# Attention and two gated layers on one core: the order of the first loads, the stores of the split sums, and 16 more dummy products

## The chip, the core and the metric

The kernel runs on one core of a Trainium2 chip. The metric is the device time of one execution in microseconds (us), here the median of the runs. TensorE (PE) multiplies matrices, VectorE (DVE), ScalarE (ACT) and GpSimd (POOL) work element by element, and SyncE (SP) issues nearly all DMAs. Each engine takes its instructions strictly in the order of its own queue, so an instruction that waits holds back all that stands behind it on its engine.

## What is computed

Attention with a bias from a running sum, then two feed-forward layers (shapes: 4 batches, 8 heads, 576 positions, 64 per head; 2304 tokens of width 512):

```python
scores = scale * np.matmul(q, k.transpose(0, 1, 3, 2))
cum = np.cumsum(np.maximum(s, 0.0), axis=-1)
bias = -(cum[:, :, :, None] - cum[:, :, None, :])
scores = np.where(causal, -1e9, scores + np.minimum(bias, 0.0))
attn = softmax(scores)                      # max, exp, sum + 1e-9
x = (attn @ v), heads side by side          # 2304 x 512
h = np.maximum(np.maximum(x @ w1, x @ w2), x @ w3); x = h @ w_out
a = x @ w_a; b = x @ w_b; out = (a * b) @ w_out2
```

## The kernel before

**Tiling.** Attention works on pairs of heads. A stage is one batch and one half of the positions (R = 0: the first 256, R = 1: the other 320), with four pairs each, so there are eight stages and 32 pairs. A pair's operands k and q are loaded with the bias as two more rows: row 64 of the k tile and row 65 of the q tile hold the running sum `cum`, so that one product per block gives scores with bias (`f_unit0`, `f_unit`, `f_joint`; the products are f and fj). The first three stages are done in this plain way. From the fourth stage on (20 pairs) q, k and `cum` are split into a rounded part and a remainder, and two products are added (`smm`); the split `cum` comes from two DRAM arrays, `kt` and `qt`, through `k_tails` and `q_tails` into the tiles KB2 and QA2.

**One pair.** TensorE makes the scores (f), DVE adds the mask and takes the maximum (L430), ACT takes the exponential (L437), DVE the reciprocal of the sum (L441, L442), POOL multiplies by it (L447), TensorE transposes the block (ft, L540), ACT copies it out (L543), TensorE multiplies with v (fpv, L563), ACT and DVE split the result into Xh and Xl (L81, L92).

**The first layer beside it.** The gates (g, L624) are matrix products of Xh and Xl with weights w1, w2, w3. Each block of weights (wraw, 512 KB) is loaded by SP (L230) into one of three buffers and then converted: ACT (L241), DVE (L244, L245), POOL (hg, L88), DVE (lg, L92). A buffer is free for the next load when its lg is done. I call the blocks W0, W1, W2 and so on in the order of their loads.

**The start.** `load_first` loads k and q of pairs 1 to 4 (kq0, 264 KB each; in the code p = 0 to 3, and tiles kraw for the first two pairs and kqv for the others), then copies the bias rows out of `cum`, one row per tile on SP's queue (L368) and one on ACT's (L369), then loads v and weights. A row's copy waits until its pair's operands have landed, since they go into the same tile. `tails` (`store_tails`, L176) then rounds `cum` (ACT, L181), takes the remainder (POOL, L182) and stores `cum` and both parts to DRAM in 15 DMAs. Ahead of all that, `spin(16)` runs 16 dummy products of the identity with itself on TensorE; two to four more stand behind each step of the first four pairs.

**What sets the order.** The code is traced with priorities, and `stream` gives every piece of attention, of the first layer and of the weights a place; a scheduler then fixes one order for each engine. `issue_after(x)` puts an instruction behind x on x's engine. A DMA has one of eight completion counters in turn and waits for the DMA that had the counter before it.

Of the kernel before, what the change touches and what calls it, by code (L numbers as in the profile page):

```python
# [8 lines left out]
F32 = mybir.dt.float32  # L9
# [20 lines left out]
def kernel(  # L30
# [18 lines left out]
    nc = tc.nc  # L49
# [10 lines left out]
    P = 128  # L60
# [7 lines left out]
    Q0 = 256  # L68
# [6 lines left out]
    def f(ap):  # L75
        return ap.bitcast(F32)
# [53 lines left out]
    SR = s.shape[0]  # L130
    ck = dram.tile([SR, 2, S], F32, name="ck")
    cq = dram.tile([SR, 2, N1], F32, name="cq")
    kt = dram.tile([SR, 2, 2, S], F32, name="kt")
    qt = dram.tile([SR, 2, 2, N1], F32, name="qt")
    x2T = dram.tile([DM, NT], F32, name="x2T")

    def pt_tile(shape, dt, nm):
# [31 lines left out]
    for h in range(2):  # L169
# [3 lines left out]
            op0=ALU.mult, op1=ALU.add,  # L173
        )

    def store_tails():  # L176
        chl = [
            mp.tile([SR, KC * N1], F32R, tag=f"X{c}1", bufs=1, name=f"c{c}")
            for c in "hl"
        ]  # L180
        nc.scalar.copy(chl[0][:, : 2 * S], cum)  # L181
        nc.gpsimd.tensor_tensor(  # L182
            chl[1][:, : 2 * S], cum, f(chl[0][:, : 2 * S]), op=ALU.subtract
        )
        for (dk, dq, t) in (
            (ck, cq, cum),
            (kt[:, 0], qt[:, 0], f(chl[0])),
            (kt[:, 1], qt[:, 1], f(chl[1])),
        ):
            a, b = parts(t)  # L190
            nc.sync.dma_start(dk[:, :, :Q0], a)
            nc.sync.dma_start(dk[:, :, Q0:], b)
            nc.sync.dma_start(dq[:, 0], b[:, 0])
            nc.sync.dma_start(dq[:, 1, 0:64], b[:, 1, 256:])
            nc.sync.dma_start(dq[:, 1, 64:], b[:, 1, :256])


    KB1 = ap_.tile([P, 2, S], F32R, name="KB1")
# [102 lines left out]
        return 2 * b + R < NPLAIN  # L301

    rows_in = []

    def pair_tiles(b, p, R):
        nk = Q0 if R == 0 else S
# [24 lines left out]
    def load_v(qv, nq, vn):  # L331
        return nc.sync.dma_start(vn, qv[:, 2 * nq :])

    def load_pair(b, p, R):

        nk = Q0 if R == 0 else S
        nq = Q0 if R == 0 else N1
        nb = 5 if R else 2
        bp = b * NP + p
        qv = (qv1 if R else qv0)[b, p]  # L340
        kt_, qt_, kn, qn, vn = pair_tiles(b, p, R)
        if is_plain(b, R):
            if R:
                nc.sync.dma_start(kn[0:66], k1[bp])
                nc.sync.dma_start(qn[0:66], q1[bp])
                nc.sync.dma_start(kn[64:65], ck[bp : bp + 1])
                nc.sync.dma_start(qn[65:66], cq[bp : bp + 1])
            else:
                load_kq0(bp, kt_)
                row = ck[bp : bp + 1, :, :Q0]  # L350
                nc.sync.dma_start(kn[64:65], row)
                nc.sync.dma_start(qn[65:66], row)
            load_v(qv, nq, vn)
        else:
            nc.sync.dma_start(qt_[:, : 2 * nq + nb * P], qv)
            for r in (0, 64):
                nc.sync.dma_start(kn[r : r + 64], kT[b, p, :, :, 0:nk])
        return kn, qn, vn.rearrange("p (b f) -> p b f", f=P)

    def load_first():  # L360

        first = [pair_tiles(0, p, 0) for p in range(NP)]
        for p in range(NP):
            load_kq0(p, first[p][0])
        for p in range(NP):
            kn, qn = first[p][2:4]
            row = parts(cum)[0][p : p + 1]
            k_ = nc.sync.dma_start(kn[64:65], row)  # L368
            q_ = nc.scalar.dma_start(qn[65:66], row)  # L369
            rows_in.append(k_.ins)  # L370
        for p in range(NP):
            with tc.issue_after(rows_in[NP - 1]):
                if p:
                    fetch_w1(w1_keys[p - 1])
                load_v(qv0[0, p], Q0, first[p][4])
        return [
            (kn, qn, vn.rearrange("p (b f) -> p b f", f=P))
            for _, _, kn, qn, vn in first
        ]
# [4 lines left out]
        return (p % 2) * (S // 2) if R == 0 else 0  # L384

    def k_tails(b, p, R):
        nk = Q0 if R == 0 else S
        ko = koff(R, p)
        nc.sync.dma_start(f(KB2[0:2, :, ko : ko + nk]), kt[b * NP + p, :, :, :nk])

    def q_tails(b, p, R):
        nq = Q0 if R == 0 else N1
        nc.sync.dma_start(
            heads(f(QA2), 2, 4, nq), (qt if R else kt)[b * NP + p, :, :, :nq]
        )

    def split_qk(b, p, R, kn, qn):
        nk = Q0 if R == 0 else S
# [297 lines left out]
    def do_split(i):  # L696
        if split_pair(i):
            b, R, p = pairs[i]
            q_tails(b, p, R)
            if not k_early(i):  # L700
                k_tails(b, p, R)
            split_qk(b, p, R, *nat_of[i][:2])

    def attn_pieces(i, X):
        b, R, p = pairs[i]
        st = {}
        out_ = []

        def add(cost, fn):
            out_.append((cost, fn))  # L710

        def nxt():
            do_split(i + 1)

        def pv():
            f_x(R, p, f_pv(R, st["PT"], nat_of.pop(i)[2]), *X())
            ahead(i + 2)

        def nop():
            pass  # L720

        plain = is_plain(b, R)
        def prep():
            st["PT"] = pt_tile([P, 2, 4 * N1], F32, "PF")

        add(0, prep)

        def do_t(u, h, pj=None):
            t_unit(st["PT"], h, u, st[u, h], pj)

        if R == 0:
            for h in range(2):
                if plain:
                    add(700, lambda h=h: st.__setitem__(h, f_unit0(*nat_of[i][:2], h, i < 4)))
                else:
                    add(550, lambda h=h: st.__setitem__(h, s_unit0(p, h)))
            if i < NP:
                add(0, lambda: spin(4))
            add(0, nxt)
            add(DLY0, nop)  # L740
            for h in range(2):
                add(330, lambda h=h: f_t0(st["PT"], h, st[h]))
                if i < NP:
                    add(0, lambda: spin(2))
            add(DLY1, nop)
            add(700, pv)
        else:
            def su(u, h):
                if plain:
                    add(900, lambda: st.__setitem__((u, h), f_unit(*nat_of[i][:2], h, u)))  # L750
                else:
                    add(600, lambda: st.__setitem__((u, h), s_unit(p, h, u)))

            add(1040, lambda: st.__setitem__("J", f_joint(*nat_of[i][:2]) if plain else s_joint(p)))
            su(2, 0)
            su(3, 0)
            su(3, 1)
            add(DLY2, nop)
            add(440, lambda: t_joint(st["PT"], st["J"]))
            add(440, lambda: do_t(2, 0, st["J"]))  # L760
            su(2, 1)
            add(0, nxt)
            add(440, lambda: do_t(3, 0))
            add(440, lambda: do_t(3, 1))
            add(330, lambda: do_t(2, 1))
            add(DLY3, nop)
            add(2200, pv)
        return out_
# [69 lines left out]
            store_tails()  # L838

    stream.append((0.1, 0, tails))  # L840
    stream.append((0.5, 0, preset))

    def w_next():
# [721 lines left out]
```

## Time and profile before

| | us |
|---|---|
| runs shown | 916.93, 917.34, 920.71 |
| median of the runs | 917.34 |
| the profiled execution's own time | 921.83 |
| span in its profile (first to last instruction) | 920.0 |
| outside the span | 1.83 |

All rows below are of the profiled execution. Its own time is 4.49 us above the median of the runs. The profile gives time from the span's start; "idle" is the time in which an engine stood still ahead of an instruction, and behind the arrow stands what ended it. TensorE's granted clock is given as a share of 2.4 GHz, so 1.00 is 2.4 and 0.50 is 1.2 GHz. A product in 32-bit floats has two records.

### The profile page before, as it was taken

Reading aid. Unit: us, or ns where it says so; the run is one execution under the profiler, and the core shown is the slowest. Engines: PE = TensorE matmul, PEld = TensorE weight load, DVE = VectorE, ACT = ScalarE, POOL = GpSimd, SP = SyncE. Lnnn points to the kernel's source line nnn. Section 1 sums busy time; section 2 is a strip of 40 time slices with the busy share of each in tenths; the row PEclk is TensorE's granted clock in tenths of the full one; section 3 lists DMA queues with packets and bytes.
Section 4 is the critical chain, followed back from the end, with each engine's and each line's share of the span. In section 5 each row is a group of like instructions: output and inputs, shape, how many; then the busy total and the mean of one; then the engine's idle time right before and its main releaser. Section 6 shows DMA issues by size and latency. Waiting matters only on the chain.

```text
span 920.0 us, 17159 instructions
## 1 busy us (share of the span) xinstructions
PE 904.3 (98%) x6296; PEld 849.0 (92%) x6296; DVE 595.9 (65%) x1407; ACT 380.7 (41%) x879; POOL 230.7 (25%) x328
## 2 busy tenths in 40 slices
PE   7999999999999999999999999999999999999998
PEld 6577889998999989999899999999999998999998
DVE  6688534555445554456469567777675868896874
ACT  4565643655446554456433332223222223423321
POOL 7554311322223222223122102111111212321211
PEclk9899999999999999999999999999999999999999
DMA  6655332213222123231134214444443234254331
GB/s 178 203 189 175 95 88 83 85 54 90 80 82 87 54 77 92 57 104 61 35 108 168 73 60 151 147 164 145 152 144 121 103 125 144 76 162 154 122 115 46
DMA packets 55212, 102.36 MB, mean 111 GB/s; under 512 B 5736, under 2 KB 39432, under 8 KB 55128
## 3 DMA queue, kind: packets, MB, share of 16 engines
q1 hardware_dynamic: 50392, 96.53, 33.3%
q10 hardware_dynamic: 4736, 4.73, 1.6%
q8 instruction: 50, 0.82, 0.4%
q14 instruction: 34, 0.28, 0.1%
HBM read 77.29 MB, written 23.94 MB: 110 GB/s over the span
## 4 chain that ended last, share of the span: by engine, by line
PE 90%; DVE 4%; DMA 3%; issue 1%; POOL 1%; ACT 1%; SPq 0%; POOLq 0%; DVEq 0%; ACTq 0%
PE g L624 24%; PE X L1111 23%; PE Z L1111 11%; PE o L652 8%; PE fpv L563 6%; PE Y L1111 6%; PE t L577 3%; PE f L498 2%; PE s L454 1%; PE s L455 1%; PE ft L540 1%; DVE slot L922 1%; DMA qvraw<-in_qv_dram 1%; PE tj L590 1%; PE fj L498 1%
## 5 line engine op out<-in xcount | busy, mean ns | idle before, releaser
L624 PE MATMUL g<-Xl,hg 128*128 128x256 f32 (+1 forms) x576 | 175.1, 305 | 0.0
L624 PE MATMUL g<-Xh,hg 128*128 128x256 f32 (+1 forms) x576 | 174.3, 305 | 0.5 <-ACT xo L657 0.5
L624 PE MATMUL g<-Xh,lg 128*128 128x256 f32 (+1 forms) x576 | 173.7, 302 | 0.0
L624 PEld LDWEIGHTS g<-Xl,hg 128*128 128x128 f32 x576 | 109.4, 190 | 4.0 <-issue 2.0
L624 PEld LDWEIGHTS g<-Xh,hg 128*128 128x128 f32 x576 | 108.9, 190 | 3.1 <-issue 0.8
L624 PEld LDWEIGHTS g<-Xh,lg 128*128 128x128 f32 x576 | 109.3, 190 | 2.0 <-issue 1.4
L1111 PE MATMUL X<-xh,wh 128*128 128x384 f32 x288 | 97.5, 339 | 1.5 <-ACT u L1154 0.6
L1111 PE MATMUL X<-xl,wh 128*128 128x384 f32 x288 | 96.9, 336 | 0.0
L1111 PE MATMUL X<-xh,wl 128*128 128x384 f32 x288 | 96.9, 337 | 0.0
L88 POOL TENSOR_SCALAR wh<-wval 128x256 fp32r<-128x256 f32 x84 | 41.7, 505 | 181.7 <-DVE wval L916 135.2
L1111 PE MATMUL X<-woh,slot 128*128 128x256 f32 x432 | 81.1, 281 | 0.5 <-ACT ob L1154 0.5
L633 DVE TENSOR_TENSOR hf<-g,hf 128x256 f32<-128x256 f32 (+1 forms) x96 | 43.6, 454 | 45.7 <-PE g L624 42.9
L447 POOL TENSOR_SCALAR P<-P,rs 128x128 f32<-128x128 f32 (+2 forms) x80 | 49.6, 624 | 88.3 <-DVE rs L442 73.3
L922 DVE TENSOR_TENSOR slot<-hraw,slot 128x768 fp32r<-128x768 f32 x60 | 60.5, 1032 | 14.9 <-POOL slot L88 14.0
L1111 PEld LDWEIGHTS X<-woh,slot 128*128 128x128 f32 x432 | 68.0, 189 | 0.7 <-ACT ob L1154 0.7
L922 DVE TENSOR_TENSOR u<-Z,u 128x384 f32<-128x384 f32 x72 | 39.6, 552 | 44.5 <-ACT u L1154 34.1
L437 ACT ACTIVATE P<-P,nm 128x128 f32<-128x128 f32 (+2 forms) x80 | 46.6, 583 | 32.9 <-DVE nm L430 26.8
L1111 PE MATMUL X<-wol,slot 128*128 128x256 f32 x216 | 60.1, 280 | 0.0
L652 PE MATMUL o<-hl,ho 128*128 128x256 f32 (+1 forms) x192 | 57.9, 303 | 0.0
L652 PE MATMUL o<-hh,ho 128*128 128x256 f32 (+1 forms) x192 | 57.6, 304 | 0.3 <-ACT xo L657 0.3
L652 PE MATMUL o<-hh,lo 128*128 128x256 f32 (+1 forms) x192 | 57.7, 304 | 0.0
L1111 PEld LDWEIGHTS X<-xh,wh 128*128 128x128 f32 x288 | 54.1, 188 | 3.0 <-ACT u L1152 1.1
(165 smaller groups left out, 2252.9 us busy)
## 6 DMA issues: line engine op xcount, KB each, us to landing
hT<-u SPq DMA_DIRECT2D x72, 192.0 KB
hraw<-hT SPq DMA_DIRECT2D x36, 384.0 KB
wraw<-in_moe_w_dram SPq DMA_DIRECT2D x18, 512.0 KB
wraw<-in_moe_w_out_dram SPq DMA_DIRECT2D x18, 512.0 KB
qvraw<-in_qv_dram SPq DMA_DIRECT2D x12, 640.0 KB
kraw<-in_kT_dram SPq DMA_DIRECT2D x24, 288.0 KB
wraw<-in_moe_w_a_dram SPq DMA_DIRECT2D x12, 512.0 KB
wraw<-in_moe_w_b_dram SPq DMA_DIRECT2D x12, 512.0 KB
```

Source lines behind the costliest of these rows:

```text
L88: nc.gpsimd.tensor_scalar(o, i, scale, 1.0, op0=ALU.mult, op1=ALU.mult)
L437: e_ = nc.scalar.activation(pt[:, c0:c1], pt[:, c0:c1], AF.Exp, bias=first, scale=-1.0, accum_out=sm[:, g : g + 1],)
L447: nc.gpsimd.tensor_scalar(pt[:, c0:c1], pt[:, c0:c1], rs[:, g : g + 1], 1.0, op0=ALU.mult, op1=ALU.mult,)
L454: nc.tensor.matmul(ps, QA1[:, qs], KB1[:, h, ksl], start=True, stop=False)
L498: nc.tensor.matmul(o, qn[0:66, h, q0 : q0 + m], kn[0:66, h, k0:k1], start=True, stop=True)
L563: nc.tensor.matmul(ps[h * D : h * D + D, c0:n], w, x, start=(t == 0), stop=(t == len(mm[h]) - 1),)
L577: nc.tensor.transpose(ps[:, j * P : j * P + P], pt[:, j * P : j * P + P], ident)
L624: nc.tensor.matmul(ps[:, :n], w[:, kk, :], x[:, kk, :], start=(i == 0), stop=(i == len(mm) - 1),)
L633: st["V"] = nc.vector.tensor_tensor(hf, ps[:, :n], hf, op=ALU.max)
L652: nc.tensor.matmul(ps[:, :n], w[:, c, :], x[:, m, :n], start=(i == 0), stop=(i == len(mm) - 1),)
L922: return {"V": nc.vector, "P": nc.gpsimd}[e].tensor_tensor(o, a, b, op=op)
L1111: nc.tensor.matmul(ps[:, :n], w, x, start=(first and i == 0), stop=(i == len(mm) - 1), skip_group_check=not first,)
```

## The change

Three things change.

1. In `load_first` the bias rows of pairs 1 and 2 are copied as soon as the operands of these two pairs and `cum` are there, and only then are the operands of pairs 3 and 4 loaded; v of pair 1 comes next, and then the rows of pairs 3 and 4.
2. `store_tails` stores only `cum` at first (5 DMAs). The two parts of the split `cum` are stored by `store_split`, later in the stream, as they lie, in one DMA each. The array `qt` is gone: `k_tails` and `q_tails` cut all they need out of `kt`, which for the twelve split pairs with R = 1 makes two DMAs of the one for KB2 and three of the one for QA2. The tails stand behind the pair's own q load.
3. After each of the first four pairs' product with v three dummy products are added, and four more in pair 5.

```diff
-    kt = dram.tile([SR, 2, 2, S], F32, name="kt")
-    qt = dram.tile([SR, 2, 2, N1], F32, name="qt")
+    kt = dram.tile([SR, 2, 2 * S], F32, name="kt")
...
+        a, b = parts(cum)
+        nc.sync.dma_start(ck[:, :, :Q0], a)
+        nc.sync.dma_start(ck[:, :, Q0:], b)
+        nc.sync.dma_start(cq[:, 0], b[:, 0])
+        nc.sync.dma_start(cq[:, 1, 0:64], b[:, 1, 256:])
+        nc.sync.dma_start(cq[:, 1, 64:], b[:, 1, :256])
+
+    def store_split():
+        with tc.issue_after(loaded_in[-1]):
+            for n in range(2):
+                nc.sync.dma_start(kt[:, n], f(chl[n][:, : 2 * S]))
...
         for p in range(NP):
+            if p == 2:
+                rows(0)
+                rows(1)
+            with ExitStack() as e_:
+                if p >= 2:
+                    e_.enter_context(tc.issue_after(rows_in[1]))
+                load_kq0(p, first[p][0])
+        with tc.issue_after(rows_in[1]):
+            load_v(qv0[0, 0], Q0, first[0][4])
+        for p in range(2, NP):
+            rows(p)
+        for p in range(1, NP):
             with tc.issue_after(rows_in[NP - 1]):
-                if p:
-                    fetch_w1(w1_keys[p - 1])
+                fetch_w1(w1_keys[p - 1])
                 load_v(qv0[0, p], Q0, first[p][4])
...
+        c = N1 + 64
+        nc.sync.dma_start(f(QA2[2:4, :N1]), b_[:, 0])
+        nc.sync.dma_start(f(QA2[2:4, c : c + 64]), b_[:, 1, 256:])
+        nc.sync.dma_start(f(QA2[2:4, c + 64 : c + N1]), b_[:, 1, :256])
...
             add(700, pv)
+            if i < NP:
+                add(0, lambda: spin(3))
...
             su(2, 0)
+            if i == NP:
+                add(0, lambda: spin(4))
...
+    stream.append((0.6, 0, store_split))
```

How the queues stand now, at the three places that matter. First ACT's queue from its start, before (F0_216 and F0_232 are the two heads of pair 1, the numbers only tell tiles apart):

```order
L369 DMA kraw_186<-cs_129 1x16x32
L369 DMA kraw_188<-cs_129 1x16x32
L369 DMA kqv_190<-cs_129 1x16x32
L369 DMA kqv_191<-cs_129 1x16x32
L181 ACT_TABLE_LOAD
L181 CAST ch_257<-cs_129 16x1152
L437 ACTIVATE F0_216,sm_219<-F0_216,nm_221 128x128
```

and with the change (L182 is the rounding of `cum` that was L181; F0_215 is F0_216's name now):

```order
L370 DMA kraw_185<-cs_128 1x16x32
L370 DMA kraw_187<-cs_128 1x16x32
L182 ACT_TABLE_LOAD
L182 CAST ch_256<-cs_128 16x1152
L370 DMA kqv_189<-cs_128 1x16x32
L370 DMA kqv_190<-cs_128 1x16x32
L455 ACTIVATE F0_215,sm_218<-F0_215,nm_220 128x128
```

The table load and the rounding moved ahead of the row copies of pairs 3 and 4; these copies still stand ahead of the first exponential.

Second, SP's queue around the weights W3 and W4, before:

```order
L195 DMA cq_107<-cs_129 16x256
L191 DMA kt_108<-ch_257 16x2x256
L192 DMA kt_108<-ch_257 16x2x320
L193 DMA qt_109<-ch_257 16x320
L230 DMA wraw_356<-in_moe_w1_dram 128x1024
L346 DMA kraw_301<-ck_106 1x1152
L346 DMA kraw_393<-ck_106 1x1152
L194 DMA qt_109<-ch_257 16x64
L230 DMA wraw_379<-in_moe_w2_dram 128x1024
L195 DMA qt_109<-ch_257 16x256
L345 DMA qvraw_302<-in_q1_dram 66x640
```

and with the change:

```order
L191 DMA cq_107<-cs_128 16x256
L231 DMA wraw_349<-in_moe_w1_dram 128x1024
L231 DMA wraw_372<-in_moe_w2_dram 128x1024
L348 DMA kraw_290<-ck_106 1x1152
L348 DMA kraw_386<-ck_106 1x1152
L347 DMA qvraw_291<-in_q1_dram 66x640
L334 DMA qvraw_291<-in_qv1_dram 128x640
L231 DMA wraw_420<-in_moe_w3_dram 128x1024
L349 DMA qvraw_291<-cq_107 1x640
```

Five stores of the split sums no longer stand among these loads, and W4 follows W3 at once.

Third, TensorE's queue from the last transposes ahead of fj to the gates behind it, before:

```order
L540 MATMUL ft0_473<-ident_90,F0_431 128x128 x3
L624 MATMUL g_975<-Xh_297,hg_0_0_142 128x256
L624 MATMUL g_1018<-Xh_297,hg_1_0_144 128x256
L498 MATMUL fj_592<-kraw_301,qvraw_302 64x288 x2
L498 MATMUL fj_595<-kraw_301,qvraw_302 64x288 x2
L624 MATMUL g_975<-Xl_298,hg_0_0_142 128x256
L624 MATMUL g_975<-Xh_297,lg_0_0_143 128x256
L624 MATMUL g_1018<-Xl_298,hg_1_0_144 128x256
```

and with the change:

```order
L150 MATMUL spin_577<-ident_90 128x128 x2
L150 MATMUL spin_594<-ident_90 128x128 x3
L516 MATMUL fj_599<-kraw_290,qvraw_291 64x288 x2
L516 MATMUL fj_602<-kraw_290,qvraw_291 64x288 x2
L150 MATMUL spin_626<-ident_90 128x128 x4
L642 MATMUL g_987<-Xh_286,hg_0_0_141 128x256
L642 MATMUL g_987<-Xl_287,hg_0_0_141 128x256
L642 MATMUL g_987<-Xh_286,lg_0_0_142 128x256
```

Dummy products took the place of gates: ahead of fj stood eight gate products before and none now, between the start and fj there are 44 dummy products in place of 32 (the 16 of the start apart), and four more stand right behind fj. From fj to the next score product (f2) there are ten gate products before and six now.

## Rows read from the trace of the kernel before

**Rows 1.** The page: TensorE's busy tenths and granted clock, 40 slices of 23 us.
```profile
PE   7999999999999999999999999999999999999998
PEclk9899999999999999999999999999999999999999
```

**Rows 2.** Stretches: length, busy us of each engine (instructions), clock, DMA share, GB/s.
```profile
10.00:20.00 10.00, 9.49 (x70) 8.53 (x69) 6.72 (x27) 7.56 (x22) 6.63 (x8) 1.00 0.84 269
42.00:60.00 18.00, 18.00 (x113) 13.09 (x112) 17.43 (x51) 12.46 (x30) 10.15 (x11) 1.00 0.52 164
```

**Rows 3.** The same view, single microseconds around the fall of the clock.
```profile
30.00:31.00 1.00, 0.12 (x2) 0.00 (x0) 1.00 (x4) 1.00 (x6) 0.85 (x1) 1.00 0.86 327
31.00:32.00 1.00, 0.34 (x2) 0.16 (x2) 1.00 (x5) 0.71 (x4) 1.00 (x3) 1.00 0.23 73
32.00:33.00 1.00, 1.00 (x6) 0.78 (x8) 1.00 (x4) 1.00 (x4) 1.00 (x2) 0.63 0.62 141
38.00:39.00 1.00, 1.00 (x4) 0.37 (x3) 0.66 (x2) 0.53 (x2) 0.40 (x1) 0.50 0.05 12
39.00:40.00 1.00, 1.00 (x5) 0.43 (x4) 0.00 (x0) 0.00 (x0) 0.24 (x1) 0.95 0.71 214
```

**Rows 4.** TensorE in order of time: start, length, operation, records, idle before.
```profile
9.68 0.68 PE L498 MATMUL f<-kraw 66*128 66x128 f32 x4 [2.43 <-DMA kqv<-cs]
...
14.82 1.50 PE L151 MATMUL spin<-ident 128*128 128x128 f32 x12
...
32.81 2.19 PE L498 MATMUL fj<-kraw,qvraw 66*64 66x288 f32 x8
...
40.76 0.91 PE L498 MATMUL f<-kraw,qvraw 66*128 66x384 f32 x2
```

**Rows 5.** SyncE in order of time: start, length, the DMAs that it issues.
```profile
5.74 1.51 SPq L368 DMA_DIRECT2D kraw<-cs  x2
7.97 1.74 SPq L368 DMA_DIRECT2D kqv<-cs  x2
...
10.39 0.42 SPq L230 DMA_DIRECT2D wraw<-in_moe_w_dram  x1
...
22.20 0.36 SPq L230 DMA_DIRECT2D wraw<-in_moe_w_dram  x1
...
23.64 0.36 SPq L230 DMA_DIRECT2D wraw<-in_moe_w_dram  x1
...
24.56 0.32 SPq L345 DMA_DIRECT2D qvraw<-in_q_dram  x1
...
30.08 0.24 SPq L347 DMA_DIRECT2D qvraw<-cq  x1
```

**Rows 6.** ScalarE in order of time.
```profile
9.76 1.28 ACT L181 ACT_TABLE_LOAD   x1 [9.76 <-DMA kqv<-cs]
...
12.17 0.40 ACT L437 ACTIVATE F<-F,nm 128x128 f32<-128x128 f32 x1
...
19.98 0.69 ACT L241 ACTIVATE wraw<-wraw 128x512 f32<-128x512 f32 x1
...
25.82 0.69 ACT L241 ACTIVATE wraw<-wraw 128x512 f32<-128x512 f32 x1 [1.85 <-DMA wraw<-in_moe_w_dram]
```

**Rows 7.** VectorE (first row) and GpSimd (the other two) in order of time.
```profile
13.19 1.75 DVE L441 TENSOR_SCALAR rs<-sm 128x2 f32<-128x2 f32 x1 [0.71 <-ACT F L437]
...
12.29 2.62 POOL L182 TENSOR_TENSOR cl<-cs,ch 16x1152 fp32r<-16x1152 f32 x1 [3.96 <-ACT ch L181]
...
30.15 1.78 POOL L447 TENSOR_SCALAR F<-F,rs 128x128 f32<-128x128 f32 x2 [1.28 <-DVE rs L442]
```

**Rows 8.** The chain that ended last, in order of time: a run of gates.
```profile
53.46 2.46 PE g L624 x19
```

**Rows 9.** A split pair later on: SyncE's tail DMA, TensorE's first joint product.
```profile
196.31 0.64 SPq L393 DMA_DIRECT2D QA<-qt  x1
...
203.68 0.38 PE L488 MATMUL sj<-KB,QA 128*128 128x288 f32 x1
```

More of the change, by code (lines that the diff above doesn't have):

```diff
@@ L174 @@
         )
+    chl = []
     def store_tails():
-        chl = [
+        chl.extend(
             mp.tile([SR, KC * N1], F32R, tag=f"X{c}1", bufs=1, name=f"c{c}")
             for c in "hl"
-        ]
+        )
         nc.scalar.copy(chl[0][:, : 2 * S], cum)
@@ L184, in store_tails @@
         )
[L185 to L195, printed above, removed]
+        a, b = parts(cum)
[8 more added lines that the diff above has]
+                nc.sync.dma_start(kt[:, n], f(chl[n][:, : 2 * S]))
     KB1 = ap_.tile([P, 2, S], F32R, name="KB1")
@@ L303 @@
     rows_in = []
+    loaded_in = []
     def pair_tiles(b, p, R):
@@ L352, in load_pair @@
                 nc.sync.dma_start(qn[65:66], row)
-            load_v(qv, nq, vn)
+            loaded_in.append(load_v(qv, nq, vn).ins)
         else:
-            nc.sync.dma_start(qt_[:, : 2 * nq + nb * P], qv)
+            loaded_in.append(nc.sync.dma_start(qt_[:, : 2 * nq + nb * P], qv).ins)
             for r in (0, 64):
@@ L362, in load_first, with rows @@
         first = [pair_tiles(0, p, 0) for p in range(NP)]
-        for p in range(NP):
-            load_kq0(p, first[p][0])
-        for p in range(NP):
+        def rows(p):
             kn, qn = first[p][2:4]
             row = parts(cum)[0][p : p + 1]
-            k_ = nc.sync.dma_start(kn[64:65], row)
-            q_ = nc.scalar.dma_start(qn[65:66], row)
-            rows_in.append(k_.ins)
+            rows_in.append(nc.sync.dma_start(kn[64:65], row).ins)
+            nc.scalar.dma_start(qn[65:66], row)
         for p in range(NP):
+            if p == 2:
[10 more added lines that the diff above has]
+        for p in range(1, NP):
             with tc.issue_after(rows_in[NP - 1]):
-                if p:
-                    fetch_w1(w1_keys[p - 1])
+                fetch_w1(w1_keys[p - 1])
                 load_v(qv0[0, p], Q0, first[p][4])
@@ L386, in k_tails @@
     def k_tails(b, p, R):
-        nk = Q0 if R == 0 else S
         ko = koff(R, p)
-        nc.sync.dma_start(f(KB2[0:2, :, ko : ko + nk]), kt[b * NP + p, :, :, :nk])
+        a, b_ = parts(kt[b * NP + p])
+        nc.sync.dma_start(f(KB2[0:2, :, ko : ko + Q0]), a)
+        if R:
+            nc.sync.dma_start(f(KB2[0:2, :, Q0:S]), b_)
     def q_tails(b, p, R):
[L392 to L395, printed above, removed]
+        a, b_ = parts(kt[b * NP + p])
+        if R == 0:
+            nc.sync.dma_start(heads(f(QA2), 2, 4, Q0), a)
+            return
+        c = N1 + 64
+        nc.sync.dma_start(f(QA2[2:4, :N1]), b_[:, 0])
+        nc.sync.dma_start(f(QA2[2:4, c : c + 64]), b_[:, 1, 256:])
+        nc.sync.dma_start(f(QA2[2:4, c + 64 : c + N1]), b_[:, 1, :256])
     def split_qk(b, p, R, kn, qn):
@@ L698, in do_split @@
             b, R, p = pairs[i]
-            q_tails(b, p, R)
-            if not k_early(i):
-                k_tails(b, p, R)
+            with tc.issue_after(loaded_in[-1]):
+                q_tails(b, p, R)
+                if not k_early(i):
+                    k_tails(b, p, R)
             split_qk(b, p, R, *nat_of[i][:2])
```

## The prediction

> **What bounds the kernel now.** I read the page's slices first: TensorE is busy in nine tenths or more of every slice but the first and the last [rows 1], and from 42 us on it has no idle time at all [rows 2]. So after 42 us the kernel takes as long as TensorE's list takes, and the change, whose new orders lie almost all ahead of that, can only move the moment at which the list runs full, and add to the list. In the first 42 us TensorE loses time in three ways. Its first score product starts at 9.68, after 2.43 us of waiting for operands [rows 4]. It stands still for most of 30 to 32 (busy 0.12 and 0.34 us) [rows 3]. And its clock then falls to half: 0.63 in the microsecond from 32, 0.95 in that from 39, 0.50 between [rows 3]. That is 0.74 + 6 + 0.1 = 6.84 us at 1.2 GHz, in which 3.4 us of work at 2.4 GHz are lost. The second reading was of what held TensorE at 30: POOL's scaling at 30.15 [rows 7], which waited for DVE, which stood behind the weights W3 and W4; ACT shows the same wait, 1.85 us for W3 at 25.82 [rows 6]. The third was SP's queue, which decides when those loads go out [rows 5].
>
> **The clock and the runs.** The profiled execution (921.83) is 4.49 us above the median. One of the three runs shown, 920.71, is 3.4 to 3.8 us above the other two, and 3.4 us is what the half-clock stretch costs. So I think it likelier than not (0.6) that the median run has no such stretch; the trace, one execution, can't show it. The Trainium skill, TensorE: Matmul & The Clock Gate, section What's actually happening, says that the chip judges TensorE's activity on a count of its own, which does not restart with the kernel, so that the same kernel can switch its clock at another point in another run; the scatter of the runs agrees, and no run here shows it directly.
>
> I compare at one place: the score product f that starts at 40.76 [rows 4], when 18 gate products are behind TensorE. At full clock it would start at 40.76 - 3.4 = 37.35. The change is 0 where it reaches this state at 40.76 (median run with the stretch) or 37.35 (without).
>
> **Part 1, the order of the first loads.** The rows of pairs 1 and 2 are issued from 5.74 as before [rows 5], when `cum` is ready, but now with nothing behind which they must wait in the queue: before, 528 KB of pairs 3 and 4 were ahead of them, and TensorE started 3.94 us after the issue. A small copy takes about 2 to 2.5 us (bounded above by the row at 30.08 and fj at 32.81: 2.7 us [rows 4, 5]). TensorE starts at about 8.0, 1.7 us earlier, between 0 and 2.4 at the ends.
>
> This gain goes no further, for ACT's queue still holds the copies of the rows of pairs 3 and 4 ahead of the first exponential. Their operands are now issued from 7.25 (5.74 + 1.51), not at 1.97. Two loads took some 2.7 us to pass (pair 2 had landed when its copy went out, at about 6.5, and pair 4 at 9.2, half a microsecond before the copies from 7.97 end at 9.71 [rows 5]); the way from issue to first byte comes on top, which no row shows apart: between 0.8 and the 2.6 of a whole small copy. They land at 10.8 to 12.5, and 0.5 us later ACT is free: 11.3 to 13.0 against 12.17 [rows 6]. I take the middle, no change. The table load (1.28) and the rounding move under this wait and cost nothing. What does get better: POOL's remainder at 12.29 (2.62 us) ends just before DVE's first L441, which took 1.75 us, is done [rows 7]; it now runs earlier and should leave 1 to 1.5 us.
>
> SP pays for it. W0 was issued at 10.39 [rows 5] and now stands behind the row of pair 4: 11.4 to 13.1, less 0.5 us for v of pair 1, which went ahead (128 KB at 269 GB/s [rows 2]). W0 to W2 land 0.5 to 2.2 us later. ACT did not wait for W2 at 19.98 [rows 6], so some of this is covered; I take 0.8 us late for the front at 20 us, which eats the 1 to 1.5 us just won.
>
> **Part 2, the stores.** W3 was issued at 22.20 and W4 at 23.64, with stores of the split sums before and between [rows 5]. Three stores directly ahead of W3 are gone, two between it and W4; at 0.3 to 0.4 us of issue each, with their counters' waits, and with the late W2 against it, W3 goes 0.1 to 1.5 us earlier, and W4, which still needs W1's buffer, within half a microsecond of 23.64. More matters that on ACT and DVE the second head of pair 3 now comes ahead of W3's conversion and not behind it: its scaling on POOL, at 30.15 before, moves to about 26 to 27, just after W3's landing. The two idle microseconds at 30 lose their cause. But fj's operands hardly move: the q load at 24.56 waits for the first product with v, and its cq row, at 30.08, waits for that load [rows 5], 5.5 us through a crowded DMA. I put the row at 28.8 to 30.2, a little earlier since fewer stores share the DMA there.
>
> Later, 12 pairs issue 3 more tail DMAs each, 36 in all. At 0.64 us [rows 9] at most they keep SP 1.9 us longer per pair. The tail at 196.31 is needed at 203.68, 7.4 us later, with 2.7 us for issue and landing of the last: I price this at 0, with 2 us in all if single tails come late. The Trainium skill, DMA: Bandwidth & Descriptors, section Rules for kernel authors, advises to coalesce small transfers, since they cost mostly overhead, which speaks against this part; by it alone the sum would be 36 x 0.64 = 23 us worse if the issues were on the path (an estimate), and the margin of 7.4 us here says that they are not.
>
> **Part 3, the dummy products.** One takes 1.50 / 6 = 0.25 us [rows 4]. Twelve lie ahead of fj, in place of eight gate products at 2.46 / 19 = 0.13 us [rows 8]. So TensorE's own list brings it to fj at 32.81 - 1.7 + 12 x 0.25 - 8 x 0.13 = 33.1, less 1.54 us idle of 30 to 32 that it fills = 31.5; if other short waits go too, 30.7. The operands allow 28.8 + 2 to 30.2 + 2.7 = 30.8 to 32.9. I take fj at 31.6, near the list's end, since both agree on it. It was at 32.81.
>
> **The sum.** From fj to f, TensorE took 7.95 us [rows 4], at full clock about 37.35 - 32.56 = 4.8 (0.25 us of the loss lie ahead of fj), ten gate products included. Now six stand there and four dummies: 4.8 - 4 x 0.13 + 4 x 0.25 = 5.3. So f comes at 36.9, with 6 gate products done and 12 owed: 12 x 0.13 = 1.56. In before's terms that is 38.45 at full clock. Against 37.35 it is **+1.1 us**, against 40.76 **-2.3 us**. In the profiled execution's own terms: 921.83 - 2.3 = 919.5 if its stretch goes. Ends of fj (30.7 to 32.9) make this -0.9 to +1.3 about the value.
>
> **Rivals.**
> Forecast: the median run of before and that of the change have the same clock: 917.34 + 1.1 = **918.4**. For it: the list is longer by 16 dummies, the operands of fj are not earlier, ACT's first exponential is not earlier. Chance 0.54 (0.40 without stretch in both, 0.14 with it in both).
> Rival A, faster: the median run of before has the stretch and the change, with TensorE kept busy through 30 to 32, has not: 917.34 - 2.3 = 915.0. For it the profiled trace; against it the runs at 916.93 and 917.34. Chance 0.27.
> Rival B, slower: the median run before has no stretch, and now TensorE waits at fj, with no gate product ahead of it to fill the wait, so that its clock falls there: 918.4 + 3.4 = 921.8. It decides from a wait like that of 30 to 32, 1.5 us in two; the operands' late end, 32.9 against a list that arrives at 30.7, makes 2.2. Chance 0.17.
> Rival C: the tails come late in the split stages, +2: 920.4. Against it the margin of 7.4 us. Chance 0.02.
> That the earlier rows do nothing for the softmax is in the forecast.
>
> **How the numbers follow.** The likeliest is 918.4. The range goes from 914.0 (A with fj early: 915.0 - 0.9, rounded) to 921.8 (B); it leaves out about half of B and a fifth of A, 0.14. A measurement of this kernel tells about 0.5%, 4.6 us, from no change: faster needs 912.7 or less, which only A with all ends favourable reaches, 0.04; slower needs 921.9, the upper half of B, 0.09; the rest, 0.87, is within.
>
> **What would show it.** Right: first score product near 8.0, first exponential at 11.3 to 13.0, W0 issued after 11.4, POOL's scaling of pair 3's second head before 27, fj at 30.7 to 32.9. Wrong: the first exponential before 11 (pairs 3 and 4 land sooner than I think, and the whole front gains); fj before 30; idle TensorE after 42 us, or tails whose products wait. If the clock falls around 32 again, the time to f tells B from the forecast.

## The result

The changed kernel took **926.2 us**, the median of six runs (920.92 to 927.22), against 917.98 for the kernel before in the same series: a ratio of 1.0077, 95% interval 1.0049 to 1.0104. It is slower by 8.2 us between the medians, 7.1 by the ratio; the prediction's range ended at 921.8. A second series (e5) gave 924.92 against 918.0, ratio 1.0076 (1.0053 to 1.0099). The profiled execution took 927.22 us, with a span of 925.4. One run of all that follow, of e8, took 1785.42 us and is left out of its median.

TensorE's slices look as before [rows 1], except that the second slice has the lower clock (0.7):

```profile
PE   7999999999999999999999999999999999999998
PEclk9799999999999999999999999999999999999999
```

The stretches that answer to [rows 2] and [rows 3], in the same columns:

```profile
10.00:20.00 10.00, 8.33 (x63) 7.50 (x61) 4.15 (x22) 3.57 (x13) 4.98 (x8) 1.00 0.73 224
42.00:60.00 18.00, 18.00 (x110) 12.20 (x108) 14.19 (x43) 11.22 (x26) 7.67 (x10) 1.00 0.64 205
22.00:23.00 1.00, 0.97 (x9) 0.78 (x7) 0.75 (x5) 0.27 (x2) 0.60 (x1) 1.00 0.78 192
23.00:24.00 1.00, 0.00 (x0) 0.00 (x0) 0.00 (x0) 0.00 (x0) 0.85 (x3) 1.00 0.61 121
24.00:25.00 1.00, 0.00 (x0) 0.00 (x0) 0.97 (x4) 0.97 (x3) 0.00 (x0) 0.66 0.20 59
...
34.00:35.00 1.00, 1.00 (x7) 0.88 (x6) 0.14 (x1) 0.00 (x0) 0.47 (x1) 0.72 0.11 45
```

TensorE now stands still in 23 to 25 and not in 30 to 32, and the clock falls there: 0.66 in the microsecond from 24, 0.50 from 25 to 34, 0.72 in the next. That is 0.68 + 9 + 0.56 = 10.2 us at 1.2 GHz, 5.1 us lost, where 3.4 were lost before. TensorE in order of time, answering to [rows 4]:

```profile
8.18 0.61 PE L516 MATMUL f<-kraw 66*128 66x128 f32 x4
...
25.14 1.11 PE L581 MATMUL fpv<-PF,qvraw 128*64 128x256 f32 x2 [2.17 <-ACT PF L561]
...
38.82 1.19 PE L516 MATMUL fj<-kraw,qvraw 66*64 66x288 f32 x8
...
43.32 0.81 PE L516 MATMUL f<-kraw,qvraw 66*128 66x384 f32 x2
```

The start came 1.5 us earlier, but fj came 6 us later. The 2.17 us at 25.14 wait for ScalarE's copy PF, and ScalarE (to [rows 6]) shows what that copy stood behind:

```profile
13.15 0.40 ACT L455 ACTIVATE F<-F,nm 128x128 f32<-128x128 f32 x1 [3.61 <-DMA kqv<-in_kq_dram]
...
24.03 0.68 ACT L242 ACTIVATE wraw<-wraw 128x512 f32<-128x512 f32 x1 [1.76 <-DMA wraw<-in_moe_w_dram]
24.61 0.47 ACT L561 COPY PF<-ft 128x384 f32<-128x384 f32 x1
```

The conversion at 24.03 is W2's; it was at 19.98. SyncE (to [rows 5]: W0, W2, a store of `cum`, W3 and W4, the q load, its cq row):

```profile
13.14 0.57 SPq L231 DMA_DIRECT2D wraw<-in_moe_w_dram  x1
...
15.18 0.43 SPq L231 DMA_DIRECT2D wraw<-in_moe_w_dram  x1
...
24.02 0.30 SPq L191 DMA_DIRECT2D cq<-cs  x1
24.77 1.18 SPq L231 DMA_DIRECT2D wraw<-in_moe_w_dram  x2
...
29.79 0.30 SPq L347 DMA_DIRECT2D qvraw<-in_q_dram  x1
...
32.70 0.24 SPq L349 DMA_DIRECT2D qvraw<-cq  x1
```

VectorE's first L459 (L441 before) takes 0.17 us and no longer 1.75, so the stall beside POOL's remainder did go; POOL's scaling of pair 3's second head (to [rows 7]) is at 30.82, later than before:

```profile
14.17 0.17 DVE L459 TENSOR_SCALAR rs<-sm 128x2 f32<-128x2 f32 x1 [3.27 <-ACT F L455]
```

```profile
30.82 1.07 POOL L465 TENSOR_SCALAR F<-F,rs 128x128 f32<-128x128 f32 x2 [2.73 <-DVE rs L460]
```

**Along the program.** I follow one product of TensorE after another through both traces and note how much later it starts with the change, each time from the span's start. At 206 us (the split stages) it is +4.03 us, at 477 +3.26, at 785 +3.23, at 840 +5.47, and so to the end. So the split stages with their single tails cost nothing, the front costs 3 to 4 us against an execution that had a half-clock stretch too, and 2.2 us arise where I had not looked at all, in the last stage. There TensorE waits in 785 to 830 (which wait, total us, times, longest), before:

```profile
PE Z L1111 <- ACT slot L81: 0.4, 1, 0.4
```

and with the change:

```profile
PE X L1135 <- DVE slot L946: 1.4, 1, 1.4
PE Z L1135 <- ACT slot L81: 1.0, 1, 1.0
```

The wait begins on VectorE, with the load hraw of a tile of the hidden layer. SyncE's issue of that load and VectorE's first instruction on it, before:

```profile
782.33 0.90 SPq L1349 DMA_DIRECT2D hraw<-hT  x2
```

```profile
786.90 0.96 DVE L922 TENSOR_TENSOR hraw<-hraw 128x768 f32<-128x768 f32 x1 [0.33 <-DMA hraw<-hT]
```

and with the change:

```profile
785.55 0.90 SPq L1373 DMA_DIRECT2D hraw<-hT  x2
```

```profile
792.37 0.96 DVE L946 TENSOR_TENSOR hraw<-hraw 128x768 f32<-128x768 f32 x1 [2.57 <-DMA hraw<-hT]
```

From issue to use it took 4.6 us before and takes 6.8 now. The order of instructions on the engines is the same there. But a load reports 16 parts, and the trace has the end of each: of this load's second half 15 had landed at 790.06, the last one at 792.24. While this half was under way went a transfer of another kind, a 16 KB piece of TensorE's own program, from 789.20 to 790.23 (the row is of the DMA queues in 789 to 790.3: packets, MB, share of 16 engines):

```profile
q8 instruction: 1, 0.02, 5.0%
```

Of such pieces there are 50 in both kernels, one for some 256 records of TensorE's queue (12,807 before: 12,592 of products and weight loads, nearly all others waits). That they are TensorE's program is read from this count. Before, the piece came at 788.75, 6.4 us behind the issue of hraw, when hraw had landed. The Trainium skill, DMA: Bandwidth & Descriptors, section Why a DMA increments its semaphore by 16 and not by 1, says that a DMA runs on up to 16 engines that finish independently, and that only the full count means landed; the 16 ends in the trace agree.

This gave a second theory: the added dummy products lengthen TensorE's program, its pieces are fetched at other moments, and one falls into a load that TensorE's chain needs.

### The profile page after: what moved, and what is told of

It is laid out like the page before. It is cut to its first block, busy times and chain, and to the rows that moved or that the text cites. A ratio compares the mean times of both kernels' runs of the same rounds, so it can differ in the third digit from the quotient of the medians.

```text
span 925.4 us, 17264 instructions
## 1 busy us (share of the span) xinstructions
PE 908.3 (98%) x6328; PEld 854.3 (92%) x6328; DVE 594.6 (64%) x1407; ACT 380.5 (41%) x879; POOL 226.7 (24%) x328
## 4 chain that ended last, share of the span: by engine, by line
PE 89%; DVE 4%; DMA 3%; issue 1%; ACT 1%; POOL 1%; SPq 1%; DVEq 0%; POOLq 0%; ACTq 0%
PE g L642 24%; PE X L1135 23%; PE Z L1135 11%; PE o L670 8%; PE fpv L581 6%; PE Y L1135 6%; PE t L595 3%; PE f L516 2%; PE s L472 2%; PE s L473 1%; DMA wraw<-in_moe_w_dram 1%; PE ft L558 1%; DVE slot L946 1%; PE tj L608 1%; PE spin L150 1%
## 5 line engine op out<-in xcount | busy, mean ns | idle before, releaser
L581 PE MATMUL fpv<-PF,qvraw 128*64 128x320 f32 (+4 forms) x432 | 55.4, 373 | 2.2 <-ACT PF L561 2.2
```

The source lines that it names most:

```text
L581: nc.tensor.matmul(ps[h * D : h * D + D, c0:n], w, x, start=(t == 0), stop=(t == len(mm[h]) - 1),)
```

## The experiments

Theory 1: the new load order makes W0 to W2 late and brings on the half-clock stretch. Theory 2: the 16 dummies cost what they take. Theory 3: stores and tails cost the time. Fourth, formed after the first four runs: the place of the program pieces. In the table, "shift" is the start of the same TensorE product in that run's profile less that in the profile of before, which holds a half-clock stretch itself, so that a kernel like it without one would stand near -3.4. Other profiles hold stretches too, of 3.4 us (e7, e8, e11), 6.8 us (e9, e16) and 10.2 us (changed, e10, e15, e18) at half clock ahead of 60 us, each worth at most half its length in the shift. A profile is one execution and can lie off its median: e1's took 920.2 us, e15's 923.38, e18's 923.48. "Piece" counts TensorE's products between the issue of hraw and the program piece behind it. The medians are of 5 to 12 runs, in e12 of two.

| run | parts | dummies at start | median us | ratio to before (95%) | shift at 206 / 785 / 840 | piece |
|---|---|---|---|---|---|---|
| before | none | 16 | 917.2 to 918.1 | | 0 | 48 |
| changed | 1, 2, 3 | 16 | 926.2 | 1.0077 (1.0049 to 1.0104) | +4.03 / +3.23 / +5.47 | 25 |
| e5 | 1, 2, 3 | 16 | 924.92 | 1.0076 (1.0053 to 1.0099) | -1.79 / -1.44 / +0.54 | 23 |
| e1 | 2, 3 | 16 | 924.58 | 1.0066 (1.0052 to 1.0080) | -1.61 / -3.10 / -1.56 | 21 |
| e2 | 1, 2 | 16 | 918.36 | 1.0008 (0.9998 to 1.0017) | -1.61 / -2.40 / -2.43 | 46 |
| e3 | 1, 3 | 16 | 919.98 | 1.0027 (1.0014 to 1.0039) | -3.05 / -3.84 / -2.41 | 26 |
| e4 | 1 | 16 | 918.78 | 1.0008 (0.9997 to 1.0018) | -1.33 / -2.83 / -2.83 | 49 |
| e6 | 3 | 16 | 922.52 | 1.0053 (1.0039 to 1.0066) | -2.02 / +0.21 / +1.57 | 21 |
| e11 | 2 | 16 | 916.14 | 0.9982 (0.9972 to 0.9991) | -5.04 / -6.53 / -6.55 | 45 |
| e7 | none | 32 | 922.64 | 1.0050 (1.0036 to 1.0064) | +1.08 / -0.49 / +1.07 | 26 |
| e12 | none | 80 | 928.67 | 1.0113 (1.0096 to 1.0131) | +7.83 / +6.24 / +6.47 | 46 |
| e13 | 2 | 32 | 920.82 | 1.0033 (1.0015 to 1.0052) | -1.66 / -2.11 / -0.75 | 20 |
| e8 | 1, 2, 3 | 1 | 919.69 | 1.0018 (1.0007 to 1.0029) | +0.02 / -0.93 / -0.94 | 42 |
| e14 | 2 | 1 | 916.4 | 0.9984 (0.9967 to 1.0002) | -5.71 / -5.80 / -5.82 | 76 |
| e15 | 1, 2 | 1 | 918.19 | 1.0004 (0.9985 to 1.0023) | +1.40 / +1.58 / +1.58 | 74 |
| e16 | 2, 3 | 1 | 921.1 | 1.0039 (1.0023 to 1.0054) | -0.11 / -0.09 / +0.04 | 43 |
| e17 | 3 | 1 | 923.18 | 1.0070 (1.0058 to 1.0083) | +1.87 / +1.08 / +1.08 | 43 |
| e18 | 1, 3 | 1 | 920.08 | 1.0031 (1.0019 to 1.0043) | +2.48 / +1.70 / +1.69 | 44 |
| e9 | 1, 2, 3, weights first | 16 | 922.63 | 1.0054 (1.0033 to 1.0074) | -0.29 / -1.09 / +0.88 | 23 |
| e10 | 1, 2, weights first | 16 | 919.11 | 1.0002 (0.9986 to 1.0018) | +0.02 / -0.70 / -0.70 | 46 |

### Which part costs: e1 to e4, e6, e11

Each takes whole parts of the change out or in. Part 1 is `load_first`:

```diff
+for p in range(NP):
+    load_kq0(p, first[p][0])
...
 for p in range(NP):
-    if p == 2:
-        rows(0)
-        rows(1)
...
```

part 3 is two lines in `attn_pieces`:

```diff
-if i < NP:
-    add(0, lambda: spin(3))
...
-if i == NP:
-    add(0, lambda: spin(4))
```

and part 2 is `store_tails`, `store_split`, `k_tails` and `q_tails` as in the diff above.

e1, the changed kernel without part 1:

> The changed kernel with the old order of the first loads (operands of all four pairs, then all rows, then W0 to W2); parts 2 and 3 stay. Theory 1 (the new load order holds back ScalarE and the weights: W0 issued 2.75 us later, W2 converted 4.05 us later, and the clock falls at 24.7 while TensorE waits for that): W0 issued near 10.4, W2 converted near 20.0, fj near 33 in place of 38.82, time 919 to 921, 5 to 7 us below the changed kernel. Theory 2 (the 16 dummy products are what costs, about 4 us): unchanged, 924 to 927. Theory 3 (the stores and tails cost the 2.2 us that appear at 807 to 829): those 2.2 us stay, so 920 to 922 together with theory 1.

e2, without part 3:

> The changed kernel without the 16 added dummy products; parts 1 and 2 stay. Theory 1 (load order): W0 issue at 13.1 and W2's conversion at 24.0 stay, fj at 37 to 39, the half-clock stretch from about 25 stays, time 924 to 927. Theory 2 (the dummies): 4 us of TensorE's list go, fj at 34 or earlier, 920 to 922. Theory 3 (stores): 924 to 927.

e3, without part 2:

> The kernel before with parts 1 and 3, that is the changed kernel with the stores and tails as they were. Theory 1 (load order): W0 to W2 late as in the changed kernel (13.1, 24.0), so 922 to 926. Theory 3 (stores and tails shift the completion counters of all later DMAs, and the output stage waits 2.2 us at 807 to 829 for it): 2.2 us less than the changed kernel, 922 to 924.5, and the shift against the kernel before is the same at 800 and at 830. Theory 2 (dummies): 924 to 927.

e4, part 1 alone:

> The kernel before with the new load order alone. Theory 1 (load order): W0 issued at 13.1, W2 converted near 24, clock at half from about 25, time 921 to 923, 3.5 to 5 us above the kernel before. Theory 2 or 3 (dummies, stores): 917 to 919, no change.

Theory 1 fell as I had put it: part 1 alone costs nothing that can be measured, and without it the changed kernel is as slow. Without part 3 nearly all is gone. e2 and e3 came out below what all three theories had. The loss at the output stage, 1.4 to 1.5 us here, is there in e1 and e3 and not in e2 and e4, so the stores (theory 3) don't make it either: e3 has the old stores.

e6, part 3 alone, and e11, part 2 alone:

> The kernel before with the 16 added dummy products alone. Theory 1 (load order) and theory 3 (stores): 917 to 919. Theory 2 (dummies): slower. In the version that the first four runs leave (the added TensorE instructions shift the 16 KB instruction loads of 1 us against the loads of the output stage, so that one of them falls into an hraw load): 1.4 to 2.2 us are lost at 800 to 830, and 0 to 1 us in the first 150 us, so 919 to 921; an instruction load starts 2.5 to 4 us behind the issue of the hraw load that DVE needs, and not 6 us as in the kernel before.

> The kernel before with the stores and tails of part 2 alone. Theory 3 (stores): slower by 2 or more, since part 2 added 4.6 to 6 us wherever part 3 was there too. Theory of the instruction loads: the TensorE program is as long as before, nothing at 800 to 830, 916.5 to 918.5.

Part 3 alone costs 4.5 us, more than any theory had. Part 2 alone **gains 2.0 us**: e11 is faster than both kernels. W3 is issued at 20.00 (22.20 before) and fj starts at 30.68 (32.81):

```profile
20.00 0.35 SPq L231 DMA_DIRECT2D wraw<-in_moe_w_dram  x1
```

```profile
30.68 1.19 PE L506 MATMUL fj<-kraw,qvraw 66*64 66x288 f32 x8
```

In e6 another 2.2 us went between 477 and 540 us: TensorE waits 1.91 us at 493.82 for ScalarE, which stood 2.72 us before a weight load:

```profile
492.77 0.69 ACT L915 ACTIVATE wraw<-wraw 128x512 f32<-128x512 f32 x1 [2.72 <-DMA wraw<-in_moe_w_b_dram]
```

Fifteen parts of that load had landed at 490.13, the last at 492.75; another program piece, of 8 KB and on another queue, went at 488.99. e5 shows the same (1.5 us), the first trace of the changed kernel doesn't. I did not test that the piece is the cause there.

### The place of the program pieces: e5, e7, e8, e12

```diff
 with tc.high_priority(5200):
-    spin(16)
+    spin(32)
```

is e7, on the kernel before; e12 has `spin(80)`; e8 has `spin(1)` on the changed kernel; e5 is the changed kernel itself.

> The changed kernel once more, as the reference for the others of this call and as another profiled execution of it. 920 to 927 by all theories; in an execution whose clock stays at 1.00 from 20 to 40 us the distance to the kernel before is about 3 us, of which 1.4 to 2.3 us arise at the output stage (800 to 830) whether or not the clock fell before.

> The kernel before with 16 more dummy products at the very start, ahead of the first score product, where TensorE has 2.43 us of waiting; nothing else is changed. Theory of the instruction loads: the TensorE program is as much longer as with part 3, so 1.4 to 2.2 us are lost at 800 to 830, 919 to 921 in all, and up to 1 us more if the dummies delay the first score product. Theory that the added PSUM tiles of part 3 shift the turn of the three buffers (no tile is added here): nothing is lost at 800 to 830, 917.5 to 918.5.

> The changed kernel with 1 dummy product at the start in place of 16; the 16 of part 3 stay. Theory of the instruction loads: the TensorE program is as long as before again, so the 1.4 to 2.2 us at 800 to 830 are gone and the instruction load starts 6 us behind the hraw load's issue, 1.4 to 2.2 us below the changed kernel of the same call (unless TensorE's clock is lower at the start for want of dummies, up to 1 us more). Theory of the PSUM tiles, or of the stores: the loss at 800 to 830 stays.

> The kernel before with 64 more dummy products at the very start. They delay the first score product by some 4 us, which is not the question. With 16 more, the instruction load that falls into the hraw load starts 2.5 to 4 us behind that load's issue, in the kernel before 6 us behind. With 64 more it should start 1 to 2 us ahead of the issue, so that no loss is left at 800 to 830 (theory of the instruction loads). Theory that the loss comes from more dummies or from a later front: 1.4 us or more are lost there again.

At the output stage all four came out as the theory of the program pieces has it. With 16 dummies at the very start and nothing else changed, hraw is late there too (e7); without 15 of them the changed kernel's wait is gone (e8); with 64 it is gone again (e12). VectorE's first instruction on hraw in e7, e8 and e12:

```profile
787.97 0.96 DVE L922 TENSOR_TENSOR hraw<-hraw 128x768 f32<-128x768 f32 x1 [1.90 <-DMA hraw<-hT]
```

```profile
785.90 0.96 DVE L946 TENSOR_TENSOR hraw<-hraw 128x768 f32<-128x768 f32 x1 [0.27 <-DMA hraw<-hT]
```

```profile
793.36 0.96 DVE L922 TENSOR_TENSOR hraw<-hraw 128x768 f32<-128x768 f32 x1 [0.56 <-DMA hraw<-hT]
```

In e12 I had the right outcome for a wrong reason. I expected the piece ahead of the issue; it came 6.1 us behind, as in the kernel before. A dummy has four records (two of the product, two weight loads), so 64 dummies make 256, one whole piece, and every later piece stands where it stood; the page of e12 counts one more:

```profile
q8 instruction: 51, 0.84, 0.4%
```

The Trainium skill, Trainium Architecture — The Big Picture, section The software stack, says that instructions are 64 bytes; 16 KB would be 256 of them (an estimate), and the count of records agrees.

Over the 20 profiles: in the eight where 20 to 26 products lie between the issue of hraw and the piece (2.8 to 3.8 us), 1.4 to 2.2 us are lost between 785 and 840; in the twelve with 42 to 76 (5.6 us or more) it is -0.05 to +0.2. In the eight the last part of the load's second half lands 1.3 to 2.2 us behind the other fifteen, in the twelve at most 0.3. So the place of the piece decides at the output stage. Why a piece that takes 1 us holds one part back by up to 2.2 us is not shown.

In total e7 costs 4.6 us, of which 1.6 arise there. It also starts later: the first score product at 11.70 in place of 9.68, later than I had allowed for, and all its runs have a mean clock of 0.994 to 0.998.

### The front: e9, e10, e13 to e18

e9 and e10 issue W0 to W2 ahead of the rows of pairs 3 and 4:

```diff
+for p in range(1, NP):
+    with tc.issue_after(rows_in[1]):
+        fetch_w1(w1_keys[p - 1])
 for p in range(2, NP):
     rows(p)
 for p in range(1, NP):
     with tc.issue_after(rows_in[NP - 1]):
-        fetch_w1(w1_keys[p - 1])
         load_v(qv0[0, p], Q0, first[p][4])
```

> The changed kernel with W0 to W2 issued right behind the rows of pairs 1 and 2 and the operands of pairs 3 and 4, ahead of the rows of pairs 3 and 4 on SyncE; ScalarE's queue is as in the changed kernel. Theory 1 (the late weights make the half-clock stretch and the slow front): W2's conversion comes before 21, the clock stays at 1.00 from 20 to 40, 921 to 923. Theory of the instruction loads (the TensorE program is as long as the changed kernel's): the loss of 1.4 to 2.2 us at 800 to 830 stays and some executions show a stretch, 921.5 to 925.

> The same order of loads without the 16 added dummy products. Theory of the instruction loads: no loss at 800 to 830; with the weights early the front is at least as good as in e2, so 916 to 918.5. Theory 1: if the late W0 to W2 still cost something in e2, 1 to 2 us below e2, 916 to 917.5.

W2's conversion came at 19.15 in e9, but the clock fell all the same, at 15 to 22 (0.56 in 15 to 20), behind 10 to 15, where TensorE was busy for only 2.77 us: it waited for VectorE, that for ScalarE, and ScalarE's queue for the operands of pairs 3 and 4. So the weights were not the only thing that can bring on a stretch, and this order is no cure: e10 had a mean clock of 0.996 or less in all its runs, and its time lies above both its expectations.

e13, e14 and e15 have 16 more or 15 fewer dummies at the start beside part 2, or parts 1 and 2:

> Part 2 alone (916.1, 2.0 us below the kernel before) with 16 more dummies at the very start. These delay the first score product by 2.0 us (11.70 in place of 9.68 in e7) and move the program loads by a quarter turn; the dummies and gates of the first pairs stand where they stood. If the extra cost of part 3 beside part 2 comes from the place of the program loads: 922 to 924.5, as in e1. If it comes from the displaced gates and dummies: the cost of e7, 4.6 us, and no more, or less, 918 to 921. Loss at 800 to 830 by both: 1.4 to 2.2 us.

> Part 2 alone with 1 dummy at the start in place of 16. TensorE waits for its first operands anyway (2.43 us before), but its clock may be lower at the first score products. If the dummies at the start are worth nothing: 915.5 to 917; if they keep the clock up: 917 to 919. No loss at 800 to 830, since the program load moves away from the hraw load (9 us behind its issue).

> Parts 1 and 2 (918.4) with 1 dummy at the start in place of 16, the control for e8. If e8's gain of 4.9 us came from the place of the program loads, these 15 dummies are worth little by themselves: 917.5 to 919.5. If it came from doing without them at the start: 913.5 to 915.

e13 stands 4.9 us higher than e11, each against its own runs of the kernel before; e7 cost 4.6. e14 and e15 are as e11 and e2: there the 15 dummies are worth nothing, so e8's gain of 5.2 us on e5 was not that of having fewer.

e16, e17 and e18 take 15 away from the other three kernels with part 3:

> Parts 2 and 3 (6.9 us above the kernel before in e1) with 1 dummy at the start in place of 16, so that the program loads stand as in the kernel before. If nearly all of e1's cost came from the place of the program loads: 0 to 1 us above the kernel before (part 2 gains 2.0, displaced dummies cost 1.5 to 2), 917 to 919. If the displaced dummies and gates cost it: 4 to 7 us above, 922 to 925.

> Part 3 alone (4.5 us above the kernel before in e6) with 1 dummy at the start. Place of the program loads: 1 to 2 us above the kernel before is left for the displaced dummies, 919 to 920, and nothing is lost at 800 to 830. Displaced dummies and gates: 3 to 4.5 us above, 921 to 922.5.

> Parts 1 and 3 (2.3 us above the kernel before in e3) with 1 dummy at the start. Place of the program loads: the 1.4 us at 800 to 830 go, 0.5 to 1.5 us above the kernel before, 918.5 to 919.5. Displaced dummies and gates: 2 us or more above, 920 or more.

The output stage loses nothing in all three, as expected, but the totals don't follow: e16 gains 3.0 us on e1 and lies between its two expectations, e17 and e18 gain nothing on e6 and e3 and stay 6.0 and 2.9 us above the kernel before. The control was not clean. With one dummy at the start the first score product takes 1.19 us (e17), with 16 it takes 0.68 (e6):

```profile
9.07 1.19 PE L498 MATMUL f<-kraw 66*128 66x128 f32 x4 [6.25 <-DMA kqv<-cs]
```

```profile
9.09 0.68 PE L498 MATMUL f<-kraw 66*128 66x128 f32 x4 [1.77 <-DMA kqv<-cs]
```

e17 does 24 records of products in 10 to 15 us, e6 does 37, both busy for all five. In kernels without part 3 this slack is lost in later waits; with part 3's longer list it isn't: e17 stands 3.89 us behind e6 at 206. What part 3 costs in the front, apart from the program pieces and the stretch, is therefore not settled.

### What brings on the stretch in the changed kernel

The two profiled executions of the same kernel, the first and e5, part in one place. In the first execution fifteen parts of W2 had landed at 21.35 and the last at 24.01; in e5 it was 20.28 and 20.64. e5 on ScalarE and on TensorE:

```profile
20.66 0.67 ACT L242 ACTIVATE wraw<-wraw 128x512 f32<-128x512 f32 x1
21.23 0.47 ACT L561 COPY PF<-ft 128x384 f32<-128x384 f32 x1
```

```profile
21.75 0.65 PE L581 MATMUL fpv<-PF,qvraw 128*64 128x256 f32 x2 [0.49 <-ACT PF L561]
...
31.27 1.19 PE L516 MATMUL fj<-kraw,qvraw 66*64 66x288 f32 x8
```

No wait of 2 us, no fall of the clock (1.00 from 20 to 40), and fj 7.5 us earlier. e18 shows the chain of the first execution again: W2's last part 2.6 us late (23.77), then

```profile
23.80 0.69 ACT L241 ACTIVATE wraw<-wraw 128x512 f32<-128x512 f32 x1 [1.74 <-DMA wraw<-in_moe_w_dram]
```

```profile
24.89 1.11 PE L573 MATMUL fpv<-PF,qvraw 128*64 128x256 f32 x2 [2.13 <-ACT PF L553]
```

and the clock at 0.50 from 25 to 30. What makes the last part late is open. A program piece lies in both intervals (from 21.15 and 22.26), but W1's last part was 1.8 us late in both too, with no piece near it, and in e5 a piece lay in W2's load as well (from 19.82), with the last part 0.36 us late. I tried no kernel that moves that alone.

The granted clock of the runs tells how often it happens: six of the changed kernel's twelve runs had a mean of 0.996 or less (924.76 to 929.42 us, median 926.8), two had 0.998 (925.09 and 925.96), and the four at 1.00 took 920.92 to 924.37, median 921.9. Of the 114 runs of the kernel before beside e1 to e18, four had 0.996 or less, 17 had 0.998 (median 918.65) and 93 had 0.999 or more (median 917.5). The two runs at 0.998 spent less time at half clock than the six and lost nearly as much, so the clock alone does not make these 5 us. That W2 is held up in each of the slower runs is not shown. Nor are late weights needed for such times: in its profile e1 issues W0 at 9.58 and converts W2 at 19.18, and three of its five runs took 924.58 to 925.15, at 0.998. That profile is of e1's fastest run and doesn't tell why.

## Why the prediction was wrong

**What held.** The first score product came at 8.18 (forecast 8.0); the first exponential at 13.15 and W0's issue at 13.14, a tenth beyond the late ends (13.0, 13.1); the 1.75 us stall went; the tails cost nothing, and part 1 as a whole neither gains nor loses. Part 2, priced at nothing, gains 2.0 us alone (e11) and adds 2.4 to 4.6 beside part 3 (e1 less e6, e5 less e3). In e5, where W2 is not held up, W3 is issued at 21.55 (forecast 20.7 to 22.1), the cq row at 29.27 (28.8 to 30.2), POOL scales pair 3's second head at 27.28 (26 to 27), and fj starts at 31.27 (31.6). At 206 us e5 stands 1.79 us ahead of the profile of before; the sum had said 2.3 ahead of an execution with the stretch. So the sum of the front was right to half a microsecond for such an execution, in part by luck: `cum` was ready 0.7 us earlier in e5 (its first rows went at 5.00, before at 5.74), and that is a difference between executions, for the first profile of the same kernel has 5.80.

**The step that failed first** is the opening one: that after 42 us the kernel takes as long as TensorE's list takes, so that the change can only move its beginning and add to it. The row that it was read from ends at 60 us [rows 2]. From 45 to 780 us the trace of before has 4.5 us of waits, all short; the largest group (total us, times, longest):

```profile
PE ft L540 <- POOL P L447: 1.1, 2, 0.6
```

At the output stage the list of the changed kernel waits 2.4 us, and whether it waits hangs on where a program piece falls. I priced a dummy at its 0.25 us; the same dummy moves every later piece of TensorE's program. That is 2.2 us in the first profile and 2.0 in e5, with no term in the sum.

**The second is the price of the late weights.** I let W0 to W2 land 0.5 to 2.2 us later and took "0.8 us late for the front". In the first profile W2's conversion came 4.05 us later. I had noted that ScalarE did not wait for W2 before; I did not follow what stands behind that conversion on ScalarE's queue: the copy PF, on which the next product of TensorE waits. SyncE's queue pays too: its store at 24.02 waited for W2's end, so W3 went at 24.77, 2.6 us later than before, where I had it up to 1.5 us earlier.

**The third is the clock.** Rival B was the right kind of case, TensorE waiting with no gate ahead to fill the gap, but I put it at fj, gave it 3.4 us and 0.17. In the profile it happens at the first product with v, and the wait and the clock together cost 5 to 6 us up to 206 (+4.03 against e5's -1.79). Half of the runs have a mean clock of 0.991 to 0.996 (0.994 in the profiled one) and take about 5 us more than those at 1.00 (926.8 against 921.9). The chance of 0.6 that the median run of before has no stretch was too low, if anything: 93 of 114 have a mean clock of 0.999 or more and only four one as low as the profiled execution's 0.996, which leaves rival A without ground.

**The sizes together.** Without a stretch the change costs 921.9 - 918.0 = 3.9 us. Against an execution of before without its 3.4 us, e5's profile loses 1.6 us up to 206 but only 0.1 up to 477, mostly since the profile of before waits 1.1 us more than e5's in between; then 1.5 at the weight load at 480 to 490, where a program piece lies in the load as well, 0.4 up to 785 and 2.0 at the output stage, 4.0 in all. So the 1.1 us of the sum for the front are met at 206 and gone later. The slower half of the runs takes some 5 more; in the profiled one that is the late W2 with its stretch.

**Open.** Why part 3 costs 4.5 us alone, 1.2 beside part 1 and 8.9 beside part 2 (e1 less e11); the program pieces explain the output stage of each, not these differences in the front.

## What to carry to other kernels

Instructions added at the start of a long program can cost more than their own time: they move the moments at which the rest of the program is fetched, and a fetch can hold back a load on a chain that has no slack. Compare the start of the same instruction along both traces before explaining a difference; it showed here that a quarter of the loss sat 780 us behind the edit. Take both from the span's start, and look in each trace for a stretch at half clock before you compare one profile with another. And when a load becomes later, read what stands behind its first user on that engine's queue, not only whether that user waited before.

## What the runs showed of the hardware

- TensorE's program comes in 16 KB pieces while the kernel runs, 50 of them, one for some 256 records of TensorE's queue, each 0.9 to 2.0 us long; at the output stage a load with a piece 2.8 to 3.8 us behind its issue had its last sixteenth 1.3 to 2.2 us behind the other fifteen (eight profiles), the others at most 0.3 (twelve).
- 64 dummies (256 records) put the pieces back where they were; 16 moved the one behind the issue of hraw from 45 to 49 products away to 20 to 26.
- Behind one dummy in place of 16 the first products of TensorE took 1.19 us and not 0.68, while the granted clock of that stretch stands as 1.00 in the profile; durations and clock row don't agree there, and I went by the durations.
- In the changed kernel's first profile the clock fell to 1.2 GHz at 24.32, within a standstill from 22.97 to 25.14, and stayed there for 10.2 us, although TensorE was busy again from 25.14 on.
